# Applying g_ln in the rounding of w_out, with a new order of steps

## The chip, the cores and the metric

One NeuronCore of a Trainium2 chip runs the whole program. The metric is the device time of one execution in microseconds (us). TensorE is PE in the profile, its weight loads are PEld, VectorE is DVE, ScalarE is ACT, GpSimd is POOL, and SP is the queue that issues all of this kernel's DMAs.

## The reference

The inputs are q, k and v (8 batches, 8 heads, 576 positions, 64 features) in fp32, and the weights w_in (512 x 1024), w_out (1024 x 512) and g_ln (1024). The weights w_in and w_out arrive as float64. Cut to what is computed:

```python
# attention, scale = 1/8, factor = 4
out_d     = softmax(scale * q_d @ k_d.T) @ v_d        # q_d, k_d, v_d: means of 4 positions
out_up    = repeat(out_d, 4, axis=position)
out_local = softmax(where(|i - j| < 4, scale * q @ k.T, -1e9)) @ v
x = (out_up + out_local) as (4608 tokens, 512)
# feed-forward
h    = x @ w_in
solu = h * softmax(h)
ln   = (solu - mean(solu)) / sqrt(var(solu) + 1e-6) * g_ln
out  = ln @ w_out                                     # (4608, 512) fp32
```

## The kernel before, in words

The eight batches go through attention one after the other: a pooled part (4 pairs of heads, steps of class `Pooled`) and a local part (5 units of windows, `Local`, or two units at once, `PairOfLocals`, from batch 3 on). Each batch adds to a tile x of 128 features x 4 pairs x 576 positions. The feed-forward part works on 36 tiles of 128 tokens: `xhl` splits x into a high and a low part, `ffn_in` makes h with 24 matmuls for either half of the 1024 columns into a PSUM tile, then takes the row maximum on DVE (`nmx`, L870), the exponential on ACT (`e`, L874), the product on DVE (L877), small statistics on POOL, and sends the result through DRAM (`u`, then `v`) so that it comes back by 32-row blocks; `ffn_ut` transposes it on DVE (L963) and splits it again (`uh` on ACT, L969, `ul` on POOL or DVE, L972); `ffn_out` makes 24 matmuls with w_out into a PSUM tile of which there is one buffer, and ACT evicts it with the token's factor (`osb`, L993). The last tile, 35, is transposed by PE (`ut`, L959) and does not go through DRAM.

PE multiplies in fp32r. For accuracy each fp32 matrix is a rounded high part and the rest as a low part: w_in is `wi_h` and `wi_l`, w_out is `wo_h` and `wo_l`. Three products are taken, high x high, high x low and low x high.

The class `Weights` makes these parts from the float64 words, in 16 pieces of 128 x 512: 0 to 7 of w_in, 8 to 15 of w_out. The generator `f32` turns a piece's words into fp32 in five rows: absolute value on ACT (L364), a clamp on DVE or POOL (L366), and three integer operations on DVE (L370, L375, L379). The generator `piece` then rounds (`hi`, ACT, L410) and subtracts (`lo`, POOL or DVE, L412). The pieces of w_out are multiplied by g_ln first, by an ACT row of its own (L409); row fc of w_out belongs to one value of g_ln, so g is a scalar for each partition.

The program is a list of steps, `plan`, numbered from 0 in the order in which the functions at the end of the kernel build it: 24 dummy matmul pairs (`keep_clock`, L1043), then each batch's steps, batch 0 followed by the 16 pieces, then tiles as their x is complete. One step is the code up to a `yield`. The table `ORDER` is a permutation of the step numbers and the program issues the steps in that order; each engine, and the SP queue, runs its own instructions strictly in the order in which they were issued. The table `OTHER` lists the steps whose instruction goes to the second engine named in `engine(usual, instead)`. So a wait on an engine holds everything that is written behind it on that engine, and the two tables set which work that is. PSUM tiles and SBUF buffers are reused in rings, which adds waits for the last reader.

## Time and profile before

| what | value |
|---|---|
| time, median of 3 runs | 589.33 us (589.28 to 589.5) |
| the profiled execution | 585.0 us, of which the span from first to last instruction 583.2 us |
| granted TensorE clock | 0.999 of full speed |
| busy share of the span | PE 97%, DVE 80%, ACT 57%, POOL 51% |
| first matmul of the feed-forward part | at 57.3 us |
| rounding of w_out's eight pieces (ACT, L410) | from 42.6 to 101.4 us |

A row of the profile names the line, engine, operation, what is written and read with buffer numbers left out, and the shape. A bracket at its end is the time for which the engine stood idle ahead of it and who ended the wait. Busy time of PE includes the dummy matmuls, and an fp32 matmul appears as two records. The chain that ended last names in order of time the work that the end of the program hung on, as far as it can be followed back.

### The profile page before, as it was taken

What the parts mean: (1) busy time and instruction counts of PE and PEld (TensorE: products, weight loads), DVE (VectorE), ACT (ScalarE), POOL (GpSimd) and SP (SyncE); (2) the same over time, 40 slices, a digit from 0 to 9 for tenths busy, and PEclk for the clock granted to TensorE, in tenths of its full rate; (3) what the DMA queues carried; (4) which work ended last, traced back from release to release, by engine and by line L of the source; (5) the groups of instructions that cost most, each with busy time, mean ns of one, the idle gap of its engine ahead of it and who ended that gap; (6) DMA issues with size and microseconds to landing.
All of it is one profiled execution on the core that took longest, in us unless ns stands there. A gap on an engine that the chain in (4) does not pass through costs nothing.

```text
span 583.2 us, 15261 instructions
## 1 busy us (share of the span) xinstructions
PE 564.1 (97%) x5852; PEld 434.1 (74%) x5852; DVE 469.3 (80%) x779; ACT 333.8 (57%) x750; POOL 299.5 (51%) x447
## 2 busy tenths in 40 slices
PE   7899998999999999999999999999999999999996
PEld 3676666777787777877777777777787777788875
DVE  7989999898988879998977967899878877545541
ACT  4778678468546646565565753466445654444442
POOL 3657677957454745648533546356433752334120
PEclk9999999999999999999999999999999999999999
DMA  8997767787877888876867976766755145304230
GB/s 280 286 213 187 189 148 193 200 193 171 228 160 185 188 191 169 194 198 157 208 153 195 228 190 167 212 157 159 195 163 148 56 145 164 127 36 163 90 110 37
DMA packets 207113, 99.59 MB, mean 171 GB/s; under 512 B 163136, under 2 KB 193344, under 8 KB 207040
## 3 DMA queue, kind: packets, MB, share of 16 engines
q1 hardware_dynamic: 207040, 98.61, 66.3%
q8 instruction: 46, 0.75, 0.6%
q14 instruction: 27, 0.22, 0.1%
HBM read 65.54 MB, written 27.79 MB: 160 GB/s over the span
## 4 chain that ended last, share of the span: by engine, by line
PE 64%; DVE 14%; SPq 7%; DMA 5%; ACT 4%; issue 3%; POOL 2%; POOLq 0%; DVEq 0%
PE o L986 27%; PE h L862 25%; SPq L286 4%; DMA v<-u 3%; PE po L844 2%; PE sd L788 2%; PE xp L753 1%; PE pdt L823 1%; PE sc L607 1%; PE sc L695 1%; DVE w L375 1%; DVE qd_flat L419 1%; DVE nmx L870 1%; SPq L942 1%; DVE e L877 1%
## 5 line engine op out<-in xcount | busy, mean ns | idle before, releaser
L986 PE MATMUL o<-wo_h,uh 128*128 128x512 f32 x288 | 116.6, 405 | 1.5 <-ACT osb L993 0.8
L862 PE MATMUL h<-wi_h,xh 128*128 128x512 f32 x288 | 116.9, 406 | 0.8 <-DVE e L877 0.6
L862 PE MATMUL h<-wi_h,xl 128*128 128x512 f32 x288 | 114.1, 396 | 0.7 <-POOL xl L1020 0.7
L986 PE MATMUL o<-wo_l,uh 128*128 128x512 f32 x288 | 113.8, 395 | 0.0
L862 PE MATMUL h<-wi_l,xh 128*128 128x512 f32 x288 | 113.7, 395 | 0.0
L986 PE MATMUL o<-wo_h,ul 128*128 128x512 f32 x288 | 78.9, 395 | 0.0
L972 POOL TENSOR_TENSOR ul<-v,uh 128x512 fp32r<-128x512 f32 x40 | 51.9, 1297 | 42.8 <-ACT uh L969 41.6
L874 ACT ACTIVATE e<-h,nmx 128x1024 f32<-128x1024 f32 x36 | 40.2, 1116 | 49.1 <-DVE nmx L870 45.5
L986 PEld LDWEIGHTS o<-wo_h,uh 128*128 128x128 f32 x288 | 54.0, 188 | 16.8 <-ACT osb L993 1.5
L862 PEld LDWEIGHTS h<-wi_h,xh 128*128 128x128 f32 x288 | 54.1, 188 | 15.8 <-issue 2.9
L862 PEld LDWEIGHTS h<-wi_h,xl 128*128 128x128 f32 x288 | 54.1, 188 | 15.4 <-POOL xl L1020 2.1
L986 PEld LDWEIGHTS o<-wo_h,ul 128*128 128x128 f32 x288 | 54.0, 188 | 13.4 <-DVE ul L972 0.3
L870 DVE TENSOR_REDUCE nmx<-h 128x1 f32<-128x1024 f32 x36 | 43.8, 1216 | 24.2 <-PE h L862 24.2
L986 PEld LDWEIGHTS o<-wo_l,uh 128*128 128x128 f32 x288 | 54.1, 188 | 12.0
L862 PEld LDWEIGHTS h<-wi_l,xh 128*128 128x128 f32 x288 | 54.1, 188 | 11.9
L877 DVE SCALAR_TENSOR_TENSOR e<-h,e 128x1024 f32<-128x1024 f32 x36 | 43.8, 1217 | 14.2 <-ACT e L874 14.0
L969 ACT ACTIVATE uh<-v 128x512 fp32r<-128x512 f32 x70 | 42.9, 624 | 18.5 <-issue 7.1
L963 DVE STREAM_TRANSPOSE v<-v 128x512 f32<-128x512 f32 x70 | 46.4, 689 | 7.6 <-DMA v<-u 7.5
L993 ACT ACTIVATE osb<-o,s 128x512 f32<-128x512 f32 x36 | 24.6, 682 | 40.0 <-PE o L986 22.1
L1020 POOL TENSOR_TENSOR xl<-x,xh 128x512 fp32r<-128x512 f32 (+1 forms) x26 | 32.9, 1268 | 22.5 <-ACT xh L1017 22.2
L487 POOL TENSOR_TENSOR vs<-vs 72x512 f32<-72x512 f32 x24 | 31.9, 1328 | 17.5 <-DMA vs<-in_v_dram 9.0
L882 POOL TENSOR_SCALAR nmu<-su 128x1 f32<-128x1 f32 x36 | 8.1, 226 | 60.1 <-DVE e L877 57.2
(128 smaller groups left out, 1116.3 us busy)
## 6 DMA issues: line engine op xcount, KB each, us to landing
u<-e SPq DMA_DIRECT2D x35, 512.0 KB
v<-u SPq DMA_DIRECT2D x140, 128.0 KB
vs<-in_v_dram SPq DMA_DIRECT2D x32, 288.0 KB
out_dram<-osb SPq DMA_DIRECT2D x36, 256.0 KB
qm<-in_q_dram SPq DMA_DIRECT2D x96, 72.0 KB
km<-in_k_dram SPq DMA_DIRECT2D x96, 72.0 KB
vw<-in_v_dram SPq DMA_DIRECT2D x80, 64.0 KB
vw<-in_v_dram SPq DMA_DIRECT2D x40, 128.0 KB
```

Of the source, the lines that this page charges most:

```text
L286: nc.sync.dma_start(t[nm][Q * 32:Q * 32 + 32, pr], src[b, 2 * pr + par, :, dh * 32:dh * 32 + 32].rearrange("(k t) d -> t k d", t=32),)
L487: eng.tensor_tensor(out=vs[:, :, 0:2 * D], in0=vs[:, :, 0:2 * D], in1=vs[:, :, 2 * D:4 * D], op=ALU.add)
L862: nc.tensor.matmul(hps[:, n, :], src[:, cc, :], wt[:, cc, n * 512:(n + 1) * 512], start=(cc == 0 and src is xh and wt is wi_h), stop=(cc = ...
L870: nc.vector.tensor_reduce(out=nmx, in_=hf, op=ALU.max, axis=AX.X, negate=True)
L874: nc.scalar.activation(e, hf, AF.Exp, bias=nmx, scale=1.0, accum_out=se)
L877: nc.vector.scalar_tensor_tensor(out=e, in0=hf, scalar=1.0, in1=e, op0=ALU.mult, op1=ALU.mult, accum_out=su)
L963: nc.vector.transpose(vg, vg)
L969: nc.scalar.activation(uh, tp, AF.Copy)
L972: (usual if v is None else engine(usual, nc.vector)).tensor_tensor(out=ul, in0=tp, in1=uh.bitcast(F32), op=ALU.subtract)
L986: nc.tensor.matmul(o, src[:, j, :], wt[:, 4 * g + j, :], start=(g == 0 and j == 0 and src is uh and wt is wo_h), stop=(g == 1 and j == 3 a ...
L993: nc.scalar.activation(osb, o, AF.Copy, scale=s)
L1020: engine(nc.gpsimd, nc.vector).tensor_tensor(out=l, in0=src, in1=h.bitcast(F32), op=ALU.subtract)
```

## The change

With `G_LATE` on, `piece` no longer scales a w_out piece in a row of its own. ACT rounds with g as the scale of the same instruction, hi = round(g * t), and one DVE operation makes the low part as lo = (t * g) - hi. The step count of a piece stays the same, so the step numbers keep their meaning. This low part has no second engine any more. The branch was in the code before and was off. `ORDER` and `OTHER` are new from the first number to the last; their rows of numbers are cut here. All line numbers behind the tables are one lower than before (L412 before is L411 after; the two new rows are L401 on ACT and L403 on DVE).

```diff
 ORDER = """
-7 192 160 6 193 194 24 195 196 197 161 162 25 163 164 8 165 198 199 166 168 167 169 170 176 12
+22 15 10 168 160 18 169 170 171 172 173 174 175 1 161 19 162 163 164 24 9 26 27 25 176 32 28 34
...
 OTHER = """
-43 91 103 178 186 199 239 242 258 266 274 356 381 423 510 517 519 543 566 574 643 685 692 695
+91 170 175 199 210 226 234 258 266 282 381 543 616 631 643 669 671 697 707 709 719 721 728 731
...
     WARM = 24
     SUMS_ON_PE = 0
-    G_LATE = False
+    G_LATE = True
     FIRST_ON_PE = ()
```

The branch that this turns on, in `piece`:

```python
                if G_LATE:
                    nc.scalar.activation(hi, t, AF.Copy, scale=g)
                    yield
                    nc.vector.scalar_tensor_tensor(
                        out=lo, in0=t, scalar=g, in1=hi.bitcast(F32), op0=ALU.mult, op1=ALU.subtract
                    )
                    yield
                    return
                nc.scalar.activation(t, t, AF.Copy, scale=g)
            nc.scalar.activation(hi, t, AF.Copy)
```

What the new tables move is seen in the engines' own rows. First DVE at the start of the program, from behind the set-up of the masks to the tenth row that works on w_in (`w_4` is piece 4, `stage` holds the words of pieces 0 and 1). Before:

```order
L366 TENSOR_SCALAR w_4_138<-w_4_138 128x512
L370 TENSOR_SCALAR w_4_138<-w_4_138 128x512
L375 SCALAR_TENSOR_TENSOR w_4_138<-w_4_131,w_4_138 128x512
L379 SCALAR_TENSOR_TENSOR w_4_138<-w_4_131,w_4_138 128x512
L366 TENSOR_SCALAR w_0_147<-w_0_147 128x512
L370 TENSOR_SCALAR w_0_147<-w_0_147 128x512
L375 SCALAR_TENSOR_TENSOR w_0_147<-stage,w_0_147 128x512
L379 SCALAR_TENSOR_TENSOR w_0_147<-stage,w_0_147 128x512
L412 TENSOR_TENSOR wi_l<-w_4_138,wi_h 128x4x4x32
```

Now:

```order
L369 TENSOR_SCALAR w_1_143<-w_1_143 128x512
L374 SCALAR_TENSOR_TENSOR w_1_143<-stage,w_1_143 128x512
L378 SCALAR_TENSOR_TENSOR w_1_143<-stage,w_1_143 128x512
L411 TENSOR_TENSOR wi_l<-w_1_143,wi_h 128x4x4x32
L365 TENSOR_SCALAR w_0_154<-w_0_154 128x512
L369 TENSOR_SCALAR w_0_154<-w_0_154 128x512
L374 SCALAR_TENSOR_TENSOR w_0_154<-stage,w_0_154 128x512
L378 SCALAR_TENSOR_TENSOR w_0_154<-stage,w_0_154 128x512
L365 TENSOR_SCALAR w_2_218<-w_2_218 128x512
```

The first piece is now piece 1. Its clamp (L365) has gone to POOL, and its low part stands directly behind its third integer row, where before four rows of piece 0 stood between the two.

The second place is on DVE around piece 10 of w_out, in the stretch before the first row maximum; `x` is the attention output of batch 0, `pl` a local softmax, `rsd` a sum's reciprocal. Before, POOL made the low part; its own rows there were:

```order
L812 TENSOR_TENSOR pd_0_875<-pd_0_875,rsd_0_1016 128x432
L366 TENSOR_SCALAR w_10_971<-w_10_971 128x512
L412 TENSOR_TENSOR wo_l<-w_8_1018,wo_h 128x512
L812 TENSOR_TENSOR pd_2_867<-pd_2_867,rsd_2_946 128x432
L812 TENSOR_TENSOR pd_1_1054<-pd_1_1054,rsd_1_1116 128x432
L412 TENSOR_TENSOR wo_l<-w_10_971,wo_h 128x512
```

DVE's rows there now:

```order
L374 SCALAR_TENSOR_TENSOR w_10_931<-w_10_929,w_10_931 128x512
L378 SCALAR_TENSOR_TENSOR w_6_869<-stage,w_6_869 128x512
L809 RECIPROCAL rsd_0_963<-smd_0_954 128x3
L378 SCALAR_TENSOR_TENSOR w_10_931<-w_10_929,w_10_931 128x512
L577 TENSOR_TENSOR x_750<-x_750,xp_1_981 128x4x116
L577 TENSOR_TENSOR x_750<-x_750,xp_2_1001 128x4x116
L403 SCALAR_TENSOR_TENSOR wo_l<-w_10_931,g_sb,wo_h 128x512
L619 TENSOR_REDUCE mxl_2_1052<-sc_2_1030 128x8
```

Two sums into x stand between the piece's last integer row and its low part, and a local row maximum waits behind it.

The third place is the end of the program on ACT, the last nine rows (`ut` is the transposed tile 35, the other `v` is tile 34, `osb` the evicted result with its factor `s`). Before:

```order
L893 ACTIVATE v_7897<-e_7864,nmu_7894 128x4x8x32
L993 ACTIVATE osb_7904<-o_7867,s_7702 128x512
L969 ACTIVATE uh_0_7917<-ut_7908 128x512
L969 ACTIVATE uh_1_7921<-ut_7908 128x512
L969 ACTIVATE uh_0_7950<-v_7851 128x512
L919 ACTIVATE e_7864,m_35_7954<-v_7897 128x1024
L993 ACTIVATE osb_7960<-o_7925,s_7899 128x512
L969 ACTIVATE uh_1_7964<-v_7851 128x512
L993 ACTIVATE osb_7993<-o_7968,s_7802 128x512
```

Now:

```order
L892 ACTIVATE v_7884<-e_7859,nmu_7881 128x4x8x32
L968 ACTIVATE uh_0_7893<-v_7876 128x512
L992 ACTIVATE osb_7896<-o_7846,s_7708 128x512
L968 ACTIVATE uh_1_7906<-v_7876 128x512
L918 ACTIVATE e_7859,m_35_7923<-v_7884 128x1024
L968 ACTIVATE uh_0_7945<-ut_7898 128x512
L992 ACTIVATE osb_7952<-o_7910,s_7768 128x512
L968 ACTIVATE uh_1_7969<-ut_7898 128x512
L992 ACTIVATE osb_7985<-o_7956,s_7886 128x512
```

Tile 34 is now split and multiplied ahead of tile 35. On PE the eight transposes of tile 35, which stood together ahead of both products, are two groups of four, one ahead of tile 34's product and one behind it.

201 rows, old and new, of tables (ORDER, OTHER) are left out of this document.

## The prediction

> **What bounds the kernel now.** First the page's totals and its span in 40 slices, since they say which engine is full and when.
>
> ```profile
> span 583.2 us, 15261 instructions
> PE 564.1 (97%) x5852; PEld 434.1 (74%) x5852; DVE 469.3 (80%) x779; ACT 333.8 (57%) x750; POOL 299.5 (51%) x447
> PE   7899998999999999999999999999999999999996
> DVE  7989999898988879998977967899878877545541
> ```
>
> PE is full nearly everywhere; the places where it is not lie at the two ends. I then cut the span into five stages by the view of busy time in windows (columns: length, busy time and instruction count of each engine, PE clock, DMA share, GB/s).
>
> ```profile
> 0.00:10.00 10.00, 6.34 (x20) 1.83 (x22) 6.92 (x18) 3.41 (x5) 1.59 (x10) 1.00 0.81 280
> 10.00:57.00 47.00, 42.19 (x871) 31.12 (x871) 43.28 (x82) 36.94 (x100) 31.44 (x27) 1.00 0.94 229
> 57.00:105.00 48.00, 45.38 (x664) 33.47 (x654) 46.83 (x81) 37.04 (x76) 36.87 (x39) 1.00 0.75 185
> 105.00:565.00 460.00, 457.30 (x4273) 358.01 (x4267) 369.01 (x598) 250.92 (x562) 228.51 (x369) 1.00 0.65 166
> 565.00:583.20 18.20, 12.84 (x57) 9.70 (x56) 3.23 (x5) 5.45 (x9) 1.12 (x4) 0.96 0.12 44
> ```
>
> From 105 to 565 us PE misses 460 - 457.3 = 2.7 us; in the last 18.2 us it misses 5.4. Ahead of 105 us it misses 105 - 93.9 = 11.1 us, and the dummy matmuls of `keep_clock` (all but one pair run there) are inside its busy time. In that early part VectorE (DVE) is busy 43.28 of 47 and 46.83 of 48 us: DVE paces the program until about 100 us, PE afterwards. All eight rounded pieces of w_out fall in the early part, and the early path crosses one of them; this is the chain that ended last, and the PE row that it leads to:
>
> ```profile
> 84.62 1.62 POOL wo_l L412
> 86.24 1.45 POOL pl L645
> ```
>
> ```profile
> 88.74 0.69 PE L665 MATMUL xp<-plT,vw 64*64 64x58 f32 x32 [1.69 <-ACT plT L263]
> ```
>
> GpSimd (POOL) writes a low part, only then normalises the local softmax, and PE stands 1.69 us. So the time is: what DVE needs to feed PE through the first 100 us, then PE's remaining work, then the tail.
>
> **The change part by part.** The prices, from the groups of instructions by shape (busy us and mean ns of one, idle time before):
>
> ```profile
> L409 ACT ACTIVATE w<-w,g_sb 128x512 f32<-128x512 f32 x8 | 5.8, 723 | 3.7 <-DVE w L379 3.7
> L410 ACT ACTIVATE wo_h<-w 128x512 fp32r<-128x512 f32 x8 | 5.1, 632 | 0.3
> L412 POOL TENSOR_TENSOR wo_l<-w,wo_h 128x512 fp32r<-128x512 f32 x7 | 9.6, 1373 | 9.4 <-ACT wo_h L410 9.3
> L412 DVE TENSOR_TENSOR wo_l<-w,wo_h 128x512 fp32r<-128x512 f32 x1 | 0.7, 684 | 0.0
> L379 DVE SCALAR_TENSOR_TENSOR w<-w,w 128x512 int32<-128x512 int32 x12 | 8.6, 719 | 0.2
> L366 POOL TENSOR_SCALAR w<-w 128x512 f32<-128x512 f32 x6 | 12.2, 2027 | 1.0 <-ACT w L364 0.8
> ```
>
> *ScalarE (ACT).* Eight scalings go; the rounding takes the scale, so it costs between 632 and 723 ns (I take the middle). ACT loses 16 x 0.68 - 8 x 0.68 = 5.4 us. It is free for 11 of the 48 us to 105, so I price this at nothing; the cover is DVE, which is fuller in the same window.
>
> *The low part.* POOL loses 7 x 1.373 = 9.6 us. DVE gets 8 operations of one pass over two SBUF tiles with a scalar. No row shows that arithmetic with this scalar, so it is bounded: 684 ns from the plain subtraction on DVE below, and above by L379, 719 ns, the same instruction kind over the same size. I take 0.72: 8 x 0.72 - 0.68 = +5.1 us on DVE, all of it in the stage that DVE paces.
>
> *The other engine choices.* Counted over the whole program, DVE goes from 745 to 735 instructions, POOL from 452 to 460 as written. The largest moves, seven normalisations `pd` and six subtractions on `pl` from DVE to POOL, are priced by
>
> ```profile
> L812 POOL TENSOR_TENSOR pd<-pd,rsd 128x432 f32<-128x432 f32 x20 | 19.0, 952 | 4.9 <-DVE rsd L810 4.0 <-DVE r L913 0.7
> L719 POOL TENSOR_TENSOR pl<-pl,mxl 128x1024 f32<-128x1024 f32 x4 | 8.6, 2146 | 3.6 <-DVE mxl L711 3.5
> L812 DVE TENSOR_TENSOR pd<-pd,rsd 128x432 f32<-128x432 f32 x12 | 7.3, 608 | 0.1
> L719 DVE TENSOR_TENSOR pl<-pl,mxl 128x1024 f32<-128x1024 f32 x6 | 7.2, 1203 | 0.1
> ```
>
> that is DVE -7 x 0.61 - 6 x 1.20 = -11.5 us and POOL +7 x 0.95 + 6 x 2.15 = +19.6; the twelve smaller moves give some back. These two moves lie behind 105 us but for one, where PE misses only 2.7 us: at most that much can be won, and as much lost again through POOL's longer rows. I enter 0, bounds -2.7 and +2.7.
>
> *The start of DVE.* This is the term that I trust most. Before, the first piece is clamped on DVE itself, straight behind ACT's first row:
>
> ```profile
> 4.52 0.67 ACT L364 ACTIVATE w<-w 128x512 f32<-128x512 f32 x1 [2.52 <-DMA w<-in_moe_w_in_dram]
> 5.22 0.43 DVE L366 TENSOR_SCALAR w<-w 128x512 f32<-128x512 f32 x1 [1.85 <-ACT w L364]
> 9.84 0.63 ACT L410 ACTIVATE wi_h<-w 128x512 fp32r<-128x512 f32 x1 [1.62 <-DVE w L379]
> ```
>
> In the new order that clamp is POOL's first row behind the set-up of the masks (2.03 us by L366), and DVE's first row of a piece waits for it: 5.2 + 2.0 = 7.2 us instead of 5.2 + 0.43. Behind it DVE stands a second time, since its fourth row is the low part of w_in's piece 1 and waits for ACT's rounding (0.63 us); before, another piece stood in between. DVE has nothing else ready at either place. Net of the one clamp it no longer does: +2.0 us, bounds +1.5 and +2.7.
>
> *What stands ahead of DVE's first results.* I counted the instructions ahead of the row maximum `nmx` of the first four token tiles on DVE, and ahead of the same tiles' first h matmul on PE, without the dummies. DVE: 109 instructions before and 114 now for tile 0, then 130 and 133, 149 and 152, 187 and 189. Two, five, five and eight of them are new low parts. Priced by their groups (most have the length of these two) the additions come to +3.4, +2.4, +1.5 and +2.0 us.
>
> ```profile
> L639 DVE TENSOR_REDUCE sml<-pl 128x8 f32<-128x520 f32 x20 | 13.6, 679 | 0.7 <-ACT pl L636 0.7
> L620 DVE TENSOR_REDUCE mxl<-sc 128x8 f32<-128x512 f32 x10 | 6.7, 675 | 0.4 <-PE sc L607 0.4
> ```
>
> The first row maximum ran here:
>
> ```profile
> 63.34 1.21 DVE L870 TENSOR_REDUCE nmx<-h 128x1 f32<-128x1024 f32 x1
> ```
>
> PE has more done by then, which must be credited. By busy time over count (an fp32 matmul shows as two records):
>
> ```profile
> L655 PE MATMUL plt<-ident,pl 128*128 128x128 f32 x80 | 12.9, 284 | 0.1
> L665 PE MATMUL xp<-plT,vw 64*64 64x58 f32 (+1 forms) x640 | 12.9, 221 | 1.7 <-ACT plT L263 1.7
> ```
>
> 0.32 us for each further `plt` and 0.04 for each `xp`: tile 2 has 8 and 16 more ahead, 3.2 us; tile 3 has 4 and 16, 1.9; tiles 0 and 1 about 2.4 and 1.5 with a few scores. Start plus DVE minus PE is 2.0 + 3.4 - 2.4 = 3.0, then 2.9, 0.3 and 2.1: about 2 us in the mean. DVE stood 3.7 us between 10 and 57 us, part of it waiting for others, and can catch up a little there: I enter +1.7, bounds -0.5 and +4.
>
> *The new wait.* POOL stood 9.3 us in front of `wo_l` for ACT's rounding, in five waits, and nobody minded. Now DVE stands there, with row maxima and scores queued behind. In the new order DVE has its own work between finishing a piece and its low part: 7.8, 5.4 and 6.2 us for three of them, but only 0.8 to 2.9 us for the other five. I enter 0 for it, and the rival below prices it.
>
> *The tail.* Now:
>
> ```profile
> 565.06 1.03 PE L959 MATMUL ut<-ident,v 128*128 128x128 f32 x8
> 566.78 0.50 PE L986 MATMUL o<-wo_h,uh 128*128 128x512 f32 x1 [0.69 <-ACT uh L969]
> 572.74 0.69 ACT L993 ACTIVATE osb<-o,s 128x512 f32<-128x512 f32 x1 [2.06 <-POOL s L926]
> 573.48 0.50 PE L986 MATMUL o<-wo_h,uh 128*128 128x512 f32 x1 [0.83 <-ACT osb L993]
> ```
>
> Two stops of PE, 0.69 and 0.83 us. The new order takes tile 34 ahead of tile 35 and puts half of the transposes of tile 35 between their two products, so that 0.45 us of PE work fills the second stop. The first remains, since the eviction of tile 33 must end. I enter -0.5, bounds -1.5 (both stops gone) and 0.
>
> *One rule against the change.* Two rows of the timeline show a DVE operation with two SBUF inputs at its plain length inside a POOL operation; a row of the view of one line (shortest, median and longest of it, in ns) shows what a collision may cost:
>
> ```profile
> 69.20 1.98 POOL L366 TENSOR_SCALAR w<-w 128x512 f32<-128x512 f32 x1
> 69.92 0.67 DVE L487 TENSOR_TENSOR vs<-vs 72x512 f32<-72x512 f32 x1
> ```
>
> ```profile
> L370 DVE TENSOR_SCALAR w<-w x16: 383/424/1886, 5.7 to 98.8; 128x512 int32<-128x512 int32 x16
> ```
>
> The Trainium skill says (SBUF — State Buffer, "Who interferes with whom") that a DVE instruction with two SBUF inputs contends with a GpSimd instruction that reads SBUF, and that the later one blocks fully. The first two rows speak against it for this pair; by the rule the sum would be that of the last rival.
>
> **Sum.** +1.7 - 0.5 + 0 + 0 = +1.2 us. The profiled execution took 585.0 us around its span of 583.2; the median of the runs is 589.33, and I add the difference to the median: **590.5 us**.
>
> **The rivals.**
>
> *A, the forecast:* DVE's later start and longer head decide; its own range is 588.8 to 593.
>
> *B, faster:* the low parts leave POOL's path. Then the 1.69 us stop at 88.74 goes, half of the 2.7 us in the middle with it, and the tail's 0.5, against 1 us left of the head: 589.33 - 1.7 - 1.3 - 0.5 + 1.0 = 586.8. For it: POOL's `wo_l` stands on the chain. Against: DVE, not POOL, is the full engine there.
>
> *C, slower still:* the wait for the rounding. 9.3 / 5 = 1.9 us a wait, of which DVE's own 0.8 to 2.9 us cover about two thirds; 0.6 us left at five places is 3 us, 590.5 + 3 = 593.5. It decides if DVE's idle time in front of the low parts passes 2 us in all.
>
> *D, the change does not reach the end:* DVE catches up wholly before 100 us, the tail stop only moves: 589.3.
>
> *E, contention:* of the eight low parts five lie ahead of the second row maximum; each longer by L370's 1886 - 424 ns gives +7.3 us: 597.8.
>
> **Chances.** A 0.48, B 0.27, C 0.12, D 0.10, E 0.03. About 0.2% (1.2 us) is what can be told from no change, and A's forecast lies on that edge: 0.26 of it counts as slower and 0.22 as same. Slower 0.26 + 0.12 + 0.03 = 0.41; same 0.22 + 0.08 = 0.30; faster 0.27 + 0.02 = 0.29. The range, 586.6 to 593.8, runs from B to C.
>
> **What would show it.** DVE's first row on a piece at 7.2 us or later and 4.9 us or less of DVE busy in the first 10 us; the first `nmx` at 66 to 69 us instead of 63.3; PE missing 12 to 14 us ahead of 105; the low parts at 0.68 to 0.75 us with little idle time before them; one tail stop under 0.5 us. The forecast is wrong if the first `nmx` comes by 64 us, if PE misses under 10 us early, or if the stretch from 105 to 565 us has gained or lost more than 2 us.

## The result: 1.3% slower, and the profile after

| | before | the change |
|---|---|---|
| median of 15 runs each | 587.6 us (583.61 to 591.52) | 594.55 us (589.82 to 599.15) |
| ratio of the change to before | | 1.0131, 95% interval 1.0105 to 1.0157 |
| profiled execution, and its span | 585.0, 583.2 us | 592.35, 590.6 us |
| granted clock, median of the executions | 0.997 (of those beside the experiments) | 0.991 |

The change costs 7.0 us at the median, where +1.2 was forecast. The time lies 0.75 us above the range, and the three runs on which 589.33 us rested were 1.7 us above the median of the fifteen; the error is therefore larger than the two times suggest. The ratio leaves out one execution of the change, which fell into a slower state (599.15 us at a clock of 0.976), and it is not the quotient of the two medians. The line numbers below are those of the change, one less than before's.

The page of the changed kernel, its totals, PE's slices and the clock granted in each slice (a 9 is 90% or more):

```profile
span 590.6 us, 15220 instructions
PE 565.4 (96%) x5852; PEld 434.4 (74%) x5852; DVE 470.9 (80%) x769; ACT 332.6 (56%) x744; POOL 302.7 (51%) x455
PE   7797899899998999999999999999999999999996
PEclk9998999999999999999999999999999999999999
```

DVE's total went from 469.3 to 470.9 us, POOL's from 299.5 to 302.7 and PE's from 564.1 to 565.4, so most of the loss is one of arrangement. PE's second, fourth and fifth slices are thinner, and in the fourth the clock is below full. The stages of the prediction, in the same view of busy time in windows (columns: length, then busy time and count of PE, weight loads, DVE, ACT, POOL, then PE's clock, DMA share, GB/s):

```profile
0.00:10.00 10.00, 6.34 (x18) 1.73 (x20) 4.22 (x13) 2.68 (x4) 3.50 (x11) 1.00 0.82 261
10.00:57.00 47.00, 40.04 (x796) 29.56 (x797) 44.83 (x78) 34.21 (x89) 27.24 (x24) 0.96 0.93 257
57.00:105.00 48.00, 45.43 (x621) 33.06 (x613) 47.15 (x84) 34.09 (x76) 35.81 (x37) 1.00 0.67 145
105.00:565.00 460.00, 454.10 (x4366) 354.96 (x4359) 367.96 (x587) 254.02 (x565) 233.40 (x374) 1.00 0.65 167
565.00:590.00 25.00, 19.49 (x86) 15.07 (x84) 6.69 (x10) 7.58 (x12) 2.77 (x11) 0.98 0.15 53
```

The middle can be cut further. The same view, first of before and then of the change:

```profile
105.00:120.00 15.00, 15.00 (x190) 11.45 (x184) 13.51 (x25) 7.30 (x13) 12.45 (x19) 1.00 0.78 188
120.00:185.00 65.00, 64.63 (x669) 50.25 (x667) 57.57 (x96) 40.67 (x94) 36.34 (x54) 1.00 0.79 183
185.00:200.00 15.00, 15.00 (x90) 11.40 (x90) 13.04 (x21) 11.21 (x36) 11.54 (x19) 1.00 0.85 205
```

```profile
105.00:120.00 15.00, 12.75 (x275) 9.98 (x268) 12.15 (x22) 7.76 (x16) 8.96 (x10) 1.00 0.73 187
120.00:185.00 65.00, 65.00 (x579) 50.95 (x579) 58.58 (x98) 40.62 (x88) 40.91 (x61) 1.00 0.83 195
185.00:200.00 15.00, 13.31 (x185) 9.90 (x184) 13.33 (x19) 8.35 (x22) 6.88 (x11) 1.00 0.79 176
```

From these windows (length less PE's busy time) and the totals comes an account of the 7.4 us between the two spans. The column on the right is the version with four repairs, told below.

| PE in us | before | change | four repairs |
|---|---|---|---|
| missing up to 105 us | 11.1 | 13.2 | 12.7 |
| missing from 105 to 200 | 0.4 | 3.9 | 3.2 |
| missing from 200 to 565 | 2.3 | 2.0 | 2.2 |
| missing behind 565 | 5.4 | 6.1 | 5.7 |
| busy | 564.1 | 565.4 | 565.7 |
| span | 583.2 | 590.6 | 589.4 |

The change's 7.4 us are 2.1 of idle time in the head, 1.4 of longer PE work, 3.2 net from 105 to 565 us and 0.7 in the tail. Between 200 and 565 us nothing more is lost.

*The head.* DVE's first rows on a piece, and POOL's clamp ahead of them, in the timeline of the change:

```profile
5.39 1.92 POOL L365 TENSOR_SCALAR w<-w 128x512 f32<-128x512 f32 x1 [3.02 <-ACT w L363]
7.35 0.43 DVE L369 TENSOR_SCALAR w<-w 128x512 int32<-128x512 int32 x1 [3.98 <-POOL w L365]
9.92 0.69 DVE L411 TENSOR_TENSOR wi_l<-w,wi_h 128x512 fp32r<-128x512 f32 x1 [0.70 <-ACT wi_h L409]
71.11 1.21 DVE L869 TENSOR_REDUCE nmx<-h 128x1 f32<-128x1024 f32 x1
```

This start is as forecast. The first h matmul, however, comes at 64.41 us instead of 57.29, and the first `nmx` at 71.11 instead of 63.34. Up to that row DVE's busy time went from 56.41 to 62.95 us: 6.5 us for five more instructions. Here is one place where the time went, in the timeline of the change:

```profile
43.04 3.05 DVE L378 SCALAR_TENSOR_TENSOR w<-w,w 128x512 int32<-128x512 int32 x1
43.49 2.05 POOL L644 TENSOR_TENSOR pl<-pl,rsl 128x512 f32<-128x512 f32 x2
54.89 2.49 POOL L644 TENSOR_TENSOR pl<-pl,rsl 128x512 f32<-128x512 f32 x2
55.08 1.40 DVE L403 SCALAR_TENSOR_TENSOR wo_l<-w,g_sb,wo_h 128x512 fp32r<-128x512 f32 x1
56.40 1.26 DVE L369 TENSOR_SCALAR w<-w 128x512 int32<-128x512 int32 x1
```

Three DVE rows lie beside POOL's products of two SBUF tiles and take 3.05, 1.40 and 1.26 us; their groups' usual lengths are about 0.69, 0.75 and 0.43. Summed over DVE's rows up to the first `nmx`, the time above the median of each row's group is 5.1 us in the change and 2.1 before. Behind the first of these rows hangs a chain:

```profile
46.12 0.72 ACT L401 ACTIVATE wo_h<-w,g_sb 128x512 fp32r<-128x512 f32 x1 [1.61 <-DVE w L378]
46.75 0.63 ACT L262 ACTIVATE x<-po 128x576 f32<-128x576 f32 x1
47.43 0.71 PE L843 MATMUL po<-pdT,vd 72*64 72x144 f32 x8 [1.51 <-ACT x L262]
48.75 1.39 PE L556 MATMUL kp<-ident,km 96*64 96x96 f32 x24 [0.61 <-DVE pdT L264]
```

ACT's rounding waits for the blocked row, ACT's copy of `po` is queued behind the rounding, and PE stands 1.51 and 0.61 us. Then PE's clock falls. The view in 5-us windows:

```profile
45.00:50.00 5.00, 2.88 (x56) 2.28 (x50) 4.79 (x10) 3.26 (x6) 4.42 (x5) 0.96 0.76 250
50.00:55.00 5.00, 4.71 (x72) 3.10 (x70) 4.03 (x7) 3.59 (x12) 3.38 (x4) 0.70 0.79 263
```

PE is busy for 2.88 of 5 us, and from 49.64 to 53.05 us, for 3.41 us, it runs at half the clock. The old order has dummy pairs at 43.6, 47.5 and 55.5 us; in the new one none stands between 43.1 and 58.3.

*The middle.* PE's waits between 105 and 200 us in the change (us in total, times, longest); before has one row in this view, of 0.2 us. The two largest:

```profile
PE po L843 <- DVE x L577: 2.8, 2, 1.5
PE xp L664 <- DMA vw<-in_v_dram: 0.4, 1, 0.4
```

PE's row at the second of the two waits for DVE, in the change:

```profile
190.01 0.71 PE L843 MATMUL po<-pdT,vd 72*64 72x144 f32 x8 [1.35 <-DVE x L577]
```

PE's rows at the first of them, before (two tiles' output matmuls between the pooled products `po` of two steps) and in the change (only scores between them):

```profile
109.69 0.71 PE L844 MATMUL po<-pdT,vd 72*64 72x144 f32 x8
110.33 0.50 PE L986 MATMUL o<-wo_h,uh 128*128 128x512 f32 x1
...
116.12 0.71 PE L844 MATMUL po<-pdT,vd 72*64 72x144 f32 x8
```

```profile
112.29 0.71 PE L843 MATMUL po<-pdT,vd 72*64 72x144 f32 x8
112.93 1.16 PE L606 MATMUL sc<-kT,qT 64*64 64x64 f32 x64
115.56 0.71 PE L843 MATMUL po<-pdT,vd 72*64 72x144 f32 x8 [1.47 <-DVE x L577]
```

*The low part and the tail.* The view of the low part's line (shortest, median and longest in ns, first and last start), and PE's rows with a wait in the last 24 us, both of the change:

```profile
L403 DVE SCALAR_TENSOR_TENSOR wo_l<-w,g_sb,wo_h x8: 743/748/1403, 55.1 to 108.7; 128x512 fp32r<-128x512 f32 x8
```

```profile
573.24 0.50 PE L985 MATMUL o<-wo_h,uh 128*128 128x512 f32 x1 [0.92 <-ACT osb L992]
580.81 0.50 PE L985 MATMUL o<-wo_h,uh 128*128 128x512 f32 x1 [1.26 <-ACT osb L992]
```

DVE never stood idle ahead of a low part. In the tail PE still stops twice, both times for the eviction, and longer than before (0.69 and 0.83).

### The profile page after: what moved, and what is told of

Same layout as the page of the kernel before. It is cut to its first block, busy times and chain, and to the rows that moved or that the text cites. A ratio compares the mean times of both kernels' runs of the same rounds, so it can differ in the third digit from the quotient of the medians.

```text
span 590.6 us, 15220 instructions
## 1 busy us (share of the span) xinstructions
PE 565.4 (96%) x5852; PEld 434.4 (74%) x5852; DVE 470.9 (80%) x769; ACT 332.6 (56%) x744; POOL 302.7 (51%) x455
## 5 line engine op out<-in xcount | busy, mean ns | idle before, releaser
L985 PEld LDWEIGHTS o<-wo_h,ul 128*128 128x128 f32 x288 | 54.1, 188 | 13.2
L899 ACT ACTIVATE e<-e,nmu 128x1024 f32<-128x1024 f32 x27 | 31.0, 1147 | 29.3 <-POOL nmu L881 29.2
L486 POOL TENSOR_TENSOR vs<-vs 72x512 f32<-72x512 f32 x27 | 36.1, 1337 | 5.5 <-DMA vs<-in_v_dram 4.9
```

What stands on the lines that cost most here:

```text
L486: eng.tensor_tensor(out=vs[:, :, 0:2 * D], in0=vs[:, :, 0:2 * D], in1=vs[:, :, 2 * D:4 * D], op=ALU.add)
L899: nc.scalar.activation(e, e, AF.Identity, bias=nmu, scale=1.0)
L985: nc.tensor.matmul(o, src[:, j, :], wt[:, 4 * g + j, :], start=(g == 0 and j == 0 and src is uh and wt is wo_h), stop=(g == 1 and j == 3 a ...
```

## The experiments

Four theories were to be told apart: the forecast's (DVE has more to do in the head and gets it done later); that POOL's products block DVE's rows of two SBUF tiles; that the granted clock takes the time; and that the new order itself, of PE or of the DMA queue, places work worse. Each run was timed beside runs of the kernel before on the same chip, whose medians were 585.07 to 587.66 us; the ratios are to these runs, formed like the one above. In edits of the tables only the lines that differ are shown.

### The form and the order apart

The form alone, in the order before, and the new order with the old form (the low parts on POOL, one of them on DVE as the table before has it):

```diff
 # e1_form: tables of before
-    G_LATE = False
+    G_LATE = True
 # e2_order: tables of the change
-    G_LATE = True
+    G_LATE = False
```

> The order and the engine choices of before, and only the form of w_out's rounding of the change: the scale inside ScalarE's rounding, all eight low parts on VectorE. Head theory (the loss comes from the order of the first 105 us, where TensorE of the change is 3.5 us behind): the form alone takes 5.4 us from ScalarE, 9.6 from GpSimd and gives VectorE about 5 to 6, at places that were not made for it; 0 to +2 us. Form theory (the eight low parts on VectorE, 849 ns each in the profile of the change instead of 720, and what queues behind them, are the loss): +4 to +8 us. Rest theory (the order behind 105 us): 0 us.

> The order and the engine choices of the change with the form of before: scale and rounding as two ScalarE rows, the low parts by GpSimd's subtraction (one of them on VectorE, as before). Head theory and rest theory: the order carries the loss, +5 to +9 us. Form theory: the loss goes with the form, 0 to +2 us.

The form alone gave 598.31 us, 1.0229 (1.0172 to 1.0285), and the order alone 608.43 us, 1.0377 (1.0333 to 1.0422). Each costs more by itself than the two together, so either table of numbers is fitted to its form: the new one is worth nothing without the new form, and the old one little with it. Differences between edited orders below are to be read with this in mind: any edit pays for the misfit that it makes.

### The head and the rest apart

Both kernels issue all 16 pieces within their first 550 steps. One kernel has the change up to there, and the steps that are left in before's order; the other the reverse.

```diff
 # e3_newhead
-ORDER = the change's
+ORDER = the change's first 550, then all others as before has them (G_LATE on)
 # e4_newrest
-ORDER = the change's
+ORDER = before's first 550, then all others as the change has them (G_LATE off)
```

> The change's first 550 steps (all dummies and all pieces of the weights, about the first 105 us) with its engine choices and its form, then what is left in the order and with the engine choices of before. Head theory: the larger part of the loss stays, +4 to +7 us (3.5 us of TensorE behind at 105 us, the rest by what follows from it). Rest theory: +1 to +3.5 us, since 3.2 us are lost between 105 and 565 us and 0.7 behind.

> The mirror image: before's first 550 steps with its engine choices and form, then what is left in the order and with the engine choices of the change. Head theory: 0 to +2 us. Rest theory: +3 to +5 us. If both halves add up, this one and the new head together give the whole +7.

The new head gave 594.48 us, 1.0147 (1.0094 to 1.0199), the same as the change. The new rest gave 597.39 us, 1.0191 (1.0145 to 1.0236). If the costs of the halves were additive they would sum to about 22 us (9.4 and 12.3 over before's 585.07), not 7, so it seems that a seam between two orders costs several us of its own. The profile of the new head shows such a cost: PE misses 3.6 us from 120 to 185 us, where the change misses nothing. So the new head together with its seam loses as much as the change; what the head alone loses, and whether the new rest is harmless, these two runs do not show.

### Three single repairs

First, the clamp of the first piece back on DVE; second, the third integer row and the rounding of piece 9 (steps 237 and 238) moved behind step 411, some fifteen places later; third, three more dummy pairs ahead of PE's early stops.

```diff
 # e5_oldstart, OTHER
-91 170 175 199 210 226 234 258 266 282 381 543 616 631 643 669 671 697 707 709 719 721 728 731
+91 175 199 210 226 234 258 266 282 381 543 616 631 643 669 671 697 707 709 719 721 728 731
 # e6_late, ORDER
-236 222 94 95 391 392 119 405 223 408 131 393 120 397 394 412 414 96 57 132 4 237 409 121 415
-159 238 82 83 89 60 410 400 142 72 413 411 61 90 97 91 416 152 73 153 401 122 98 123 402 403
+236 222 94 95 391 392 119 405 223 408 131 393 120 397 394 412 414 96 57 132 4 409 121 415 159
+82 83 89 60 410 400 142 72 413 411 237 238 61 90 97 91 416 152 73 153 401 122 98 123 402 403
 # e7_fill, in the loop that issues the steps
+    extra = {72: 2, 416: 1}
...
+        for x in range(extra.get(now[0], 0)):
+            keep_clock(f"{n}_{x}")
```

> The change with one engine choice undone: the clamp of the first piece of w_in is VectorE's again (0.43 us) instead of GpSimd's (1.92 us in the profile of the change), so VectorE's first row of a piece comes at about 5.9 us instead of 7.35. Start theory (VectorE's late start is what the head loses): first row maximum 1.5 us earlier, time 1.5 us less than the change or more. Contention-and-clock theory (the head loses by VectorE standing 2.39 us in front of a busy GpSimd at 43 us, by what queues behind that, and by TensorE's halved clock): 0 to -1 us against the change.

> The change with two steps moved: the last operation on piece 9 (two SBUF inputs; 3.05 us at 43.04 in the profile of the change, against 0.66 elsewhere) and ScalarE's scaled rounding behind it stand behind three reductions and a reciprocal of VectorE that were queued behind them. Contention theory: that operation falls to under 1.2 us, ScalarE's copy of the pooled product to x comes 1.5 us earlier, TensorE's 1.51 us stop at 47.4 goes, and so does the half-clock window of 3.41 us at 49.6; first row maximum about 2 us earlier, time 2 to 4 us less than the change. Start theory: no more than 0.5 us, since what VectorE saves it loses at the next wait.

> The change with three more pairs of dummy matmuls (0.46 us each): two ahead of the pooled product that TensorE waited 1.51 us for at 47.4, one ahead of the transposes that waited 0.61 us. Nothing else is moved. Clock theory (TensorE's idle time there makes the clock fall to half for a window of 3.41 us, in which it does half the work): no half-clock window in the early part, TensorE's work ahead of 105 us up by 1.5 us, time 1 to 2 us less than the change. If the idle time alone costs and not the clock: 0 to +0.5 us.

The old start gave 593.53 us, 1.0112 (1.0066 to 1.0157). DVE began 2 us earlier and the first `nmx` came at 70.80 us, only 0.3 earlier: the late start is taken up before that row.

The moved rows gave 591.31 us, 1.0089 (1.0056 to 1.0121), 2 to 3 us less than the change. In its timeline the row is still blocked, but for less, and `po` on PE no longer waits behind its rounding (PE waits 1.93 us for `pdT` there instead, and a half-clock stretch of 3.41 us still follows, at 50.57):

```profile
45.86 1.72 DVE L378 SCALAR_TENSOR_TENSOR w<-w,w 128x512 int32<-128x512 int32 x1
```

DVE's busy time up to the first `nmx` fell from 62.95 to 61.60 us, but that row did not move (71.15).

The dummies gave 592.72 us, 1.0123 (1.0076 to 1.0169). The view in 5-us windows shows that they did their work in the head, PE full from 45 to 50 us and the clock whole; the profile's one half-clock stretch ahead of the last matmul is elsewhere, 6.83 us from 188.69:

```profile
45.00:50.00 5.00, 4.94 (x63) 2.84 (x63) 4.79 (x10) 3.11 (x7) 4.42 (x5) 1.00 0.85 231
50.00:55.00 5.00, 4.18 (x90) 3.17 (x90) 4.00 (x7) 3.87 (x14) 3.01 (x3) 1.00 0.99 279
```

The first and the third repair are within the interval of the change's own ratio (1.0105 to 1.0157). The second is outside of it, but its own interval reaches into it.

### The price of a collision

A kernel of its own measures the disputed cost: eight operations of 128x512 on DVE, with or without eight on POOL beside them, all tiles but one in SBUF and nothing to wait for. It leaves the computation out; its output is a copy of a part of q.

```diff
+    phases = (
+        ("A", low, None), ("B", None, tt), ("C", low, tt), ("D", reduce, tt),
+        ("E", clamp, tt), ("F", low, ts), ("G", add_bank, tt), ("H", reduce, ts),
+    )
```

Here `low` is the low part's operation, `clamp` a clamp, `reduce` a sum over 64 columns and `add_bank` a sum of an SBUF and a PSUM tile, all on DVE; `tt` is POOL's product of two tiles and `ts` its clamp of one.

> No attention and no FFN in it (the output is only a copy of an input): the disputed cost alone. Eight operations in each stretch, all 128x512: VectorE's low part (two SBUF inputs and a scalar) alone, GpSimd's product alone, then both at once; then beside GpSimd's product VectorE's reduction, its clamp, and its sum of an SBUF and a PSUM tile; then the low part and the reduction beside GpSimd's clamp (one input). Contention theory: low part alone about 0.70 us, beside GpSimd's product much longer (it waits for one product at a time, 1 to 2 us a piece), the reduction and the PSUM sum at their plain length. If the long rows of the profile had another cause: under 0.8 us everywhere.

The groups by shape (busy us, mean ns of one, idle time before them), and the view of the low part's line:

```profile
L47 DVE SCALAR_TENSOR_TENSOR dveC<-a,g,b 128x512 f32<-128x512 f32 x8 | 12.6, 1570 | 0.3
L63 POOL TENSOR_TENSOR poolC<-c,d 128x512 f32<-128x512 f32 x8 | 12.2, 1529 | 0.5
L63 POOL TENSOR_TENSOR poolB<-c,d 128x512 f32<-128x512 f32 x8 | 10.1, 1262 | 0.5
L55 DVE TENSOR_SCALAR dveE<-a 128x512 f32<-128x512 f32 x8 | 10.0, 1249 | 0.2
L59 DVE TENSOR_TENSOR dveG<-a,bank 128x512 f32<-128x512 f32 x8 | 5.5, 685 | 0.2
L51 DVE TENSOR_REDUCE dveD<-a 128x8 f32<-128x512 f32 x8 | 5.5, 684 | 0.2
```

```profile
L47 DVE SCALAR_TENSOR_TENSOR dveA<-a,g,b x8: 750/752/752, 6.5 to 12.0; 128x512 f32<-128x512 f32 x8
L47 DVE SCALAR_TENSOR_TENSOR dveC<-a,g,b x8: 752/1660/1867, 25.1 to 37.1; 128x512 f32<-128x512 f32 x8
L47 DVE SCALAR_TENSOR_TENSOR dveF<-a,g,b x8: 752/752/1173, 61.3 to 67.9; 128x512 f32<-128x512 f32 x8
```

The low part costs 752 ns alone, 1660 at the median beside POOL's product and 752 beside POOL's clamp, where three of the eight are longer (977, 1173 and 1173); the product itself goes from 1262 to 1529 ns. The clamp on DVE is blocked as well (1249 ns where the change's trace has 0.43 us for that shape), while the reduction (684) and the sum with PSUM (685) are not. So the rows in the prediction that spoke against a collision, POOL's L366 beside DVE's L487, were of a kind that mostly does not collide here; POOL's L645, the product, is of the kind that does.

### Is it the load of the low parts?

The change without its eight low parts, TensorE reading `wo_h` where it would read `wo_l`; beside it the change once more.

```diff
 # e9_nolow
-                    nc.vector.scalar_tensor_tensor(
-                        out=lo, in0=t, scalar=g, in1=hi.bitcast(F32), op0=ALU.mult, op1=ALU.subtract
-                    )
...
-                            o, src[:, j, :], wt[:, 4 * g + j, :],
+                            o, src[:, j, :], wo_h[:, 4 * g + j, :],
```

> The change without its eight low parts: VectorE's 6.8 us of them (8 x 849 ns in the profile of the change) are left out, and TensorE reads the rounded part in their place, so that it does as much work as before (the output is therefore less exact). Head theory (what VectorE has ahead of its first row maxima paces the program): tile 0's row maximum 2 us earlier, tile 3's 5 to 6, time 4 to 6 us less than the change. If the loss lies in the order of the other engines: 0 to -1.5 us.

> The changed kernel once more, as it is, beside the three others, for a time from the same chip and a second profile. Clock theory: its executions again spread over 589 to 599 us with the mean granted clock, and a second profile has its half-clock windows at other places than 49.6 us, each behind a stop of TensorE; executions at full clock come to about 590.5 us, 6.5 above those of the kernel before (584).

Without the low parts 594.68 us, 1.0143 (1.0093 to 1.0193); the change again 594.49 us, 1.0142 (1.0102 to 1.0183). Leaving out the low parts wins nothing at the median. But the granted clock was lower without them (0.9855 at the median against 0.9895), and at a like clock they seem to count for about 1 us: at 0.993 two executions took 591.5 and 591.9 us, where the change took 592.7 at 0.993 and 593.2 at 0.994. Both profiles have PE at half clock for 13.65 us in the head. The page's clock row of the change's second profile:

```profile
PEclk9996899999999999999999999999999999999999
```

The same kernel had 3.4 us of it in its first profile, and the time was still 593.09 us here against 592.35 there.

### PE's stop at 114 us, and the repairs together

In the change PE waits 1.47 us at 114 for DVE's sum into x, which is queued behind two transposes of a feed-forward tile that came late. Steps 521 and 522 were moved ahead of 328; then this and the three repairs were joined.

```diff
 # e11_xfirst, ORDER (e12_four: this and the three edits above)
-519 310 492 690 691 347 324 425 692 325 520 328 521 329 330 891 331 332 522 311 713 714 312 677
+519 310 492 690 691 347 324 425 692 325 520 521 522 328 329 330 891 331 332 311 713 714 312 677
```

> The change with two steps moved, the pooled product of the second batch's last pair and VectorE's sum of it into x: they stand ahead of the two transposes in front of which VectorE waited 2.05 us for a transfer at 111.5. TensorE's stop of 1.47 us at 114 waited for that sum. If TensorE paces the program behind 105 us, a stop taken away there comes back whole: the stop gone and 1 to 1.5 us less than the change. If the lag of the head sets everything behind it: the stop goes and a later one takes its place, 0 to -0.5 us.

> Four repairs of the change together: the first clamp on VectorE again, piece 9's last operation behind the reductions, three pairs of dummies in front of two stops, the sum into x ahead of the transposes. If the causes are separate: 1.1 + 2.8 + 0.7 + 1 = 5 to 6 us less than the change, so within 3 us of before. If they are one lag that each of them shows: 3 to 4 us less than the change.

The single edit gave 594.37 us, 1.0157 (1.0103 to 1.0211). Its wait was replaced at once by another, of 0.91 us ahead of 115.94 us, for another row of DVE (`pl`, L624): what is late is the DVE queue there, not one row. All four together gave **590.47 us**, 1.0069 (1.0030 to 1.0108), 4.0 us less than the change on the same chip. PE's rows in the head, over 57 and 48 us, show no half clock:

```profile
0.00:57.00 57.00, 46.49 (x812) 31.07 (x816) 48.72 (x92) 37.16 (x93) 28.23 (x34) 1.00 0.90 257
57.00:105.00 48.00, 45.78 (x626) 33.46 (x616) 47.16 (x85) 33.81 (x76) 36.71 (x37) 1.00 0.68 148
```

Its ratio is the lowest of the changed versions, though its interval overlaps that of the moved rows alone, and it is still slower than before. Two more kernels asked what is left in it: one without the low parts (the edit of e9), one with the low part of piece 9 and the rows of piece 10 (steps 239 and 241 to 245) behind step 125.

```diff
 # e14_four_later, ORDER
-101 102 240 241 242 113 103 485 243 114 244 213 486 126 133 8 245 264 124 125 134 135 136 214
+102 240 113 103 485 114 213 486 126 133 8 264 124 125 239 241 242 243 244 245 134 135 136 214
```

> The change with the four repairs, and without the eight low parts (TensorE reads the rounded part twice, so the output is not the reference's): the run without them alone had TensorE's clock at half for 13.65 us around 55 us, which hid what VectorE saved. Load theory (VectorE's 6.8 us of low parts set the first FFN products): first h product 2 to 3 us earlier than 64.1, 3 to 5 us less than the four repairs alone. Order theory (the first h products wait for what the new order has ahead of them on TensorE, ScalarE and VectorE, whoever does the low parts): first h product at 63 us or later, 0 to -1.5 us.

> The change with the four repairs, and with the first low part and four operations on w_out's piece 10 moved behind the two sums into x that token tile 0 needs. Order theory: VectorE's chain from 53 to 62 us loses 2.8 us of them (0.74 + 0.42 + 0.43 + 2 x 0.69, less what is given back by other waits), the first h product starts 1.5 to 2.5 us earlier than 64.1, time 1 to 2 us less than the four repairs alone. Load theory: the same work is only done later, within 0.5 us.

Without the low parts 592.67 us, 1.0113 (1.0074 to 1.0153). The first h came at 61.30 us, 2.8 earlier than with them, but the fourth tile's `nmx` at 117.89 against 118.06, and the end no earlier. This is the strongest evidence against the forecast's mechanism: DVE relieved of some 6 us in the head, the first result 3 us earlier, and nothing gained. It is not without a gap. In this profile the third tile's `nmx` is still 3.9 us earlier (89.08 against 93.03), and the lead goes behind it, where PE runs at half clock for 6.83 us from 102.70. The executions tell the same at a like clock, though: 592.2 and 593.4 us at 0.996 and 0.997, against 590.1 to 594.4 for five executions of the four repairs there. The later piece 10 gave 593.35 us, 1.0115 (1.0074 to 1.0155), with the first h at 65.32, not earlier, behind a half-clock stretch of 3.41 us at 61.17: moving these rows gained nothing either.

### The DMA queue

In the change the SP queue stands for 6.9 us behind one load of `vw` that waits for a buffer, between 50 and 57 us; before, its longest wait between 20 and 115 us is 1.7. That load (step 724) was moved behind step 700, in the change and in the version with four repairs.

```diff
 # e17_sp and e18_four_sp, ORDER (the lines between are the same, one place to the left)
-246 247 143 144 145 451 288 452 453 248 432 154 433 224 225 215 724 249 250 289 251 419 493 494
+246 247 143 144 145 451 288 452 453 248 432 154 433 224 225 215 249 250 289 251 419 493 494 495
...
-385 699 337 700 537 687 760 761 578 884 762 672 706 376 707 749 579 708 562 763 906 924 709
+385 699 337 700 724 537 687 760 761 578 884 762 672 706 376 707 749 579 708 562 763 906 924 709
```

> The change with one step moved: the load of the third batch's last window of v. In the change its four transfers stand early on SP's queue and hold one of the five vw buffers from about 50 us until that batch needs it behind 150 us; here the step stands where before has it, behind the same batch's other early windows. Buffer theory: SP's wait of 6.9 us for TensorE's first xp product (50.4 to 57.3 us in the profile of the change) falls under 2 us, all later transfers come some 5 us earlier, TensorE's waits for vw at 105 to 108 us go, the row maximum of tile 3 comes at 112 to 115 us instead of 119.2; time 3 to 6 us less than the change. If VectorE's load or the order of the other engines sets the loss: SP's wait goes, the time stays within 1 us.

> The change with the four repairs and with the same load of v moved. Buffer theory: 2 to 4 us less than the four repairs alone, so within 2 us of before at the same granted clock. If the two sets of repairs mend the same lag: within 1 us of the better of the two.

They gave 594.7 us, 1.0148 (1.0101 to 1.0195), and 591.62 us, 1.0102 (1.0072 to 1.0133). The waits of SP in the first of them, over the same window:

```profile
SPq L304 <- PE xp L664: 6.8, 1, 6.8
SPq L909 <- ACT e L899: 5.7, 1, 5.7
```

The next load of the same line stands in its place, and a second long wait appears. The theory fell: the early load did not cost the time.

### A lag put into the kernel before

The last question was what a late head costs by itself, and whether dummies help the kernel before. Six reductions of 0.68 us went onto DVE ahead of step 114; apart from that, four dummy pairs into the head.

```diff
 # e15_before_lag
+        if now[0] == 114:
+            idle = small.tile([P, 4], F32, name="idle", bufs=1)
+            for _ in range(6):
+                nc.vector.tensor_reduce(
+                    out=idle, in_=ident.unsqueeze(1).broadcast_to([P, 4, P]), op=ALU.add, axis=AX.X
+                )
 # e16_before_fill
+    extra = {437: 3, 408: 1}
...
+        for x in range(extra.get(now[0], 0)):
+            keep_clock(f"{n}_{x}")
```

> The kernel before with one thing added: six reductions of a constant tile on VectorE (0.68 us each, 4.1 us, results unused) ahead of the first sum into x at 53.4 us, so that token tile 0 and all behind it is late by that much. Lag theory (the time follows the start of the first FFN products): first h product 3.5 to 4 us later than 57.3, time +3.5 to +5, more where the clock falls too. If TensorE's slack ahead of 105 us takes it up: 0 to +2 us.

> The kernel before with four pairs of dummy matmuls added: three ahead of the xp products that TensorE waited 1.69 us for at 88.7, one ahead of the transposes at 36.1. Clock theory: executions of before spread from 583.5 to 593 us with the mean granted clock (0.986 to 1.0), because one window or more at half speed falls behind these stops in some of them; with the dummies more of them run at full clock, the median falls by 0.5 to 1.5 us towards 584. If the spread has another source: the same median within 0.5 us.

With the lag the first h came 3.8 us later (61.06) and the first `nmx` 4.9 (68.22), and the time was 588.55 us, 1.0047 (1.0014 to 1.0080), 2.8 us more. The fourth tile's `nmx` came at 117.13 us instead of 111.65, nearly as late as in the change (119.19). The granted clock was 0.988 at the median instead of 0.997, and at a like clock the version with the lag is no slower than the kernel before: seven executions at 0.985 to 0.988 have a median of 589.8 us, six of before at 0.986 to 0.988 one of 591.5. So this lag costs what it takes from the clock, and nothing more that can be seen. The change's loss is there at full clock too (below), so a late head by itself does not account for it. The dummies gave 586.57 us, 1.0033 (0.9998 to 1.0069): no gain, so nothing here beats the kernel before.

## Why the prediction was right in its direction and wrong in its size and mechanism

Three steps failed. The middle was entered at 0 within 2.7 us either way, and 3.2 us were lost there. The granted clock, lower by 0.006 at the median, had no term. And DVE's longer head, the term that made the forecast positive, was counted at plain row lengths and taken to set the end, which the runs that took it back do not bear out. That the direction came out right is therefore in part luck.

*The start of DVE (+2.0).* Right as an event: DVE's first row on a piece came at 7.35 us (forecast 7.2 or later), and DVE was busy for 4.22 us of the first 10 (4.9 or less). Wrong as a cost: undoing it moved the first `nmx` by 0.3 us and the time by 1 us, inside the interval. It was "the term that I trust most".

*What stands ahead of DVE's first results (+3.4 less 2.4 for tile 0).* This step failed. It counted instructions at plain lengths: up to the first `nmx` DVE's busy time grew by 6.5 us, not 3.4. Of that 3.0 is time above the plain length (5.1 less 2.1), in its largest rows beside POOL's products; the 3.5 that are left are what the count gave. The first `nmx` came at 71.11 us, outside the 66 to 69 that were forecast. PE's missing time ahead of 105 us, 13.2, is inside the 12 to 14 that were forecast, and 2.1 us more than before is near the term's 1.7; but the version with four repairs and no low parts shows that this agreement is not evidence for the mechanism: with DVE's load taken back the end came no earlier.

*The granted clock.* It was not in the sum at all. The change's stop at 46 us, with no dummy near it, lets the clock fall, and its PE work is 1.4 us longer in the profiled execution. Over the executions the time goes with the granted clock (correlation -0.88 over 83 executions of before, -0.81 over 14 of the change). Lines through them give 584.0 us at full clock for before and 591.2 for the change, rising by 564 and 360 us for each unit of clock lost. By these slopes the 0.006 between the median clocks is 2.2 to 3.4 us, and at full clock most of the loss remains: 7.2 us by the two lines. The change's executions at 0.998 or above are only three, in its two series, 589.82, 591.28 and 594.26 us, against a median of 584.1 for before. With four repairs the five such executions have a median of 590.1. So of the 4.0 us that the repairs won on one chip about 1 is left at a like clock; the rest came with the clock, which rose from 0.9895 to 0.9975 at the median.

*The middle (0, bounds -2.7 and +2.7).* This is the largest miss: 3.2 us lost, outside of the bound and past the 2 us that the prediction itself named as the sign of being wrong. The step priced engines' busy times and took the 2.7 us that PE missed as what could be gained or lost. But PE was full from 105 to 120 and from 185 to 200 us because the order before had matmuls of a tile standing between two dependent attention steps. The new order has two `po` with DVE's sum between them at 115 and at 190 us, and PE stands 1.47 and 1.35 us; the rows at the first place show it. The second stop stands in all twelve profiles that keep the new order there (1.35 to 1.59 us), no repair touched it, and in seven of the twelve a half-clock stretch of 3.41 or 6.83 us begins at its end or just behind it, at 188.7 to 195.2 us. A bound taken from today's idle time holds only while the order that fills it stays.

*The low part (8 x 0.72).* The price alone is 752 ns by measurement, above the bound of 719 that was taken from L379; in the kernel the median is 748 and the longest 1403. They were 1 us dearer in all than forecast, and it did not matter. The forecast of little idle time ahead of them was right, so rival C, the new wait, did not occur.

*The tail (-0.5).* The wrong sign, +0.7: both stops stayed and became longer, 0.92 and 1.26 us instead of 0.69 and 0.83. The four transposes stand between the two products and run, but the eviction ahead of the last product ends that much later than they do; whether the order of the tiles or the place of ACT's rows does this was not tried.

*The rivals.* E (597.8) forecast 8.5 us over 589.33, the difference nearest to the measured 7.0, while C (593.5) was nearest in time; neither for the right reason. Of E's low parts only one of eight was blocked for long (1403 ns; the next is 883). Its mechanism is nevertheless the one that the sum should have held, with another victim: the conversion rows of the pieces, and through them ACT's queue and PE. The Trainium skill's rule that was weighed there (SBUF — State Buffer, "Who interferes with whom") agrees with the measurement for POOL's two-tile product (1660 against 752 ns), and mostly not for POOL's clamp of one SBUF tile (752 at the median, three of eight longer). The prediction set the rule aside on two rows of a kind that mostly escapes it.

*What is settled and what is not.* Shown: form and order are of use only together; the early load, piece 10's place and DVE's late start do not set the loss; the four repairs, of the collision, the clock, the start and the wait at 114, are worth about 4 us together, most of it by the clock. Likely, with the gaps named above: DVE's low parts and the late head do not set it. Seen in the trace but not shown by an undoing: the stops of PE at 105 to 120 and at 185 to 190 us, since moving one wait away brought up the next and the second stop was not tried. Open: why the four repairs still stay about 6 us behind at full clock. Their account above names where (1.6 us of idle head, 2.8 from 105 to 200 us, 1.6 of PE work, nearly all of it the dummies), not what one would have to change.

## What to carry to other kernels

When a new order comes with an edit, price the order: look for places where a full engine is full only because another tile's work stands between two dependent steps, and for stops of TensorE that have lost their dummy matmuls. Before a two-input DVE row is priced at its plain length, look at what POOL does beside it, and with which operands; a row from another pair of operations proves nothing. An engine's added load is a cost only if undoing it moves the end. And a repair is to be credited at a like granted clock, since a version can win several us by the clock alone.

## What the runs showed of the hardware

The clock falls in steps: every stretch at half clock ahead of the last matmul in these profiles lasted 3.41 us or a multiple (6.83, 10.24, 13.65), the same kernel had one of 3.41 and one of 13.65 at the same place in two executions, and in the change it begins behind stops of 1.51 and 0.61 us. By the line for the kernel before, a window of 3.41 us (0.0058 of the span at half clock, 0.0029 of mean clock) is worth about 1.6 us. The Trainium skill (TensorE: Matmul & The Clock Gate, "Part 1: The HAM clock gate") describes windows of this length with full and half clock only, and free of the program's start, which agrees: the clock first comes to full anywhere from 6.56 to 9.71 us behind the first instruction, and all later changes lie whole windows from there. That stops well short of a window in all are enough, with PE busy for 2.88 of 5 us around them, is what this trace adds. Over the nineteen profiles of the whole kernel it can be told more closely. All 33 such stretches begin behind a window in which PE was busy for 2.25 us or less, no window with more was followed by one, and of 35 windows with 2.0 us or less 27 were. So it matters how the windows lie over a stop, which fits the one of 1.35 to 1.59 us near 190 us that brought a half-clock stretch in seven profiles of twelve.

A collision on SBUF slows both engines (DVE's 752 ns to 1660 at the median, POOL's 1262 to 1529 in the mean), and POOL's products in a row can keep one DVE row waiting through more than one of them: 3.05 us for a row of 0.69.
